# An attention, mixture and gated-unit kernel on one core: the first gated unit's product scheme is changed

## The chip, the core and the metric

The kernel runs on one core of a Trainium2 chip. The metric is the device time of one execution in microseconds (us), median of several. The core has five engines that each take their own row of instructions in order and wait for each other through semaphores: TensorE (PE, matmuls into PSUM banks), VectorE (DVE), ScalarE (ACT), GpSimd (POOL) and SyncE (SP, which issues the DMAs).

## What is computed

```python
attn_out = _attn_ref(q, k, v)         # (2, 8, 576, 64), local band plus a pooled path
x = attn_out.transpose(0, 2, 1, 3).reshape(1152, 512)
x = _moe_ref(x, w_gate, w1, w2)       # 8 experts, 512 -> 1024 -> 512, relu
a = x @ w_a                           # 512 -> 1536
b = x @ w_b
return a * b @ w_out                  # 1536 -> 512
```

All of it is float32. The change touches the last three lines, the gated layer.

## The kernel before

A float32 product is made of three reduced-precision ones: each operand is split into a high part and the rest (`xh`, `xl` for tokens, `hi`, `lo` of a weight block), and hi·hi, hi·lo and lo·hi are added up in PSUM.

The 1152 tokens are handled in two chunks of 512 and 640 columns (`CN` is half of each: 256 and 320). The experts' 16 half units and the gated layer's 6 units follow one another; each unit makes its hidden values with 256 + 256 weight columns and then adds its share of the output, one output tile for each 128 tokens (`o_tile`, `o_mm`).

A unit's first product is a 2x2 block product, with the weights in blocks of depth and columns and the tokens in blocks B11, B12, B21, B22. `g_chunk` does it with seven products in the Strassen-Winograd manner (`PRODUCTS`): combinations of the weight blocks (A11, S1 to S4, A12, A22, made by `queue_combined` on POOL) times blocks or combinations of the tokens (T1 to T4, made by `combine_x`). T2, T3 and T4 lie in `Th`, `Tl`; T1 overwrites the place of B12 in `xh`, `xl`. The results are put together by DVE from PSUM banks and buffers `G`; for a gated unit `a` and `b` are multiplied, and the product is split into `gh` (ACT) and `gl` (POOL).

Between the experts and the gated layer the accumulators are transposed by PE (`t_step`), split into `xh` and `xl`, and kept unsplit as well (tiles `xh_`, `xl_`, `xt_` in the instruction lists), from which `transposed` queues the sums T1 to T4 of each chunk. Before, the second chunk's sums are queued in two parts, one ahead of the last tile's transposes and one after them.

The order of the work is set while the program is written out. PE's products are written in order; between them `pump` takes tasks from queues (`tq` the sums, `wq` the weight pieces, `dq` an earlier decoding), as a small model of the engines' times allows, and each engine executes its row in the order that results. Weight blocks lie in a ring of 13 slots; a slot is used again when its block's uses are done. Raw weights pass through two staging buffers (`raw`), and the next load is issued when a buffer's last use is written out. An eviction of a result frees its PSUM bank; the products of a unit go round six banks, the output tiles round two.

Of the kernel before, what the change touches and what calls it, by code (L numbers as in the profile page):

```python
# [8 lines left out]
F32 = mybir.dt.float32  # L9
# [4 lines left out]
ALU = mybir.AluOpType  # L14
# [5 lines left out]
def attn_moe_glu_kernel(  # L20
# [134 lines left out]
    def run(q):  # L155
        t = q.pop(0)
        t.fn()
        return t
# [75 lines left out]

    def queue_plain(u):

        u.w = {}
        rs = halves(u.load1, (2, 2))
        for i in range(2):
            for j in range(2):  # L240
                def piece(i=i, j=j):
                    b = u.w[i, j] = new_block(NB * 2)
                    split(b, rs[j].tile[:, :, 256 * i:256 * i + 256], 2)
                    rs[j].used()
                wq.append(Task(piece, 0.68, ready=rs[j].ready, slot=True))
# [370 lines left out]
    def g_chunk(u, c, glu=False):  # L616
# [44 lines left out]
        for a, b, bk in PRODUCTS:  # L661
# [47 lines left out]
            yield  # L709


    PLACES = {5: (1, 2, 3, 4, 5), 4: (1, 3, 4, 5), 3: (1, 4, 5)}
# [7 lines left out]
    def phase(u, c, tiles, glu=False, places=None):  # L720

        places = places or PLACES[len(tiles)]
        for i, _ in enumerate(g_chunk(u, c, glu)):
            gate_step()
            for t, at in zip(tiles, places):
                if at == i:
                    t()
                    gate_step()
# [382 lines left out]
    with tc.manual_schedule():  # L1111
# [59 lines left out]
        def close_attention():  # L1171
# [20 lines left out]
            for u in glu_g:  # L1192
                queue_combined(u)
                queue_out(u, 2)
# [135 lines left out]

        def transposed(c, part=None):
            x0, x1 = keep[c]
            where = {"t1": x0[:, 0:2], "b12": x1[:, 0:2], "b22": x1[:, 2:4], "b21": x0[:, 2:4]}
            tq.extend(combine_x(c, lambda name: where[name], (v, g, g, v), None, part))

        for t, tt in enumerate(TILES[1]):
            o_tile(units[last], 1, t)
# [6 lines left out]
            else:  # L1344
                for _ in t_step(TILES[1][t - 1], keep):
                    pass
                if t == 4:
                    transposed(1, slice(0, 192))
        while tq:
            run(tq)  # L1350

        def last_step():
            for _ in t_step(TILES[1][-1], keep, "o"):
                pass
            transposed(1, slice(192, 320))

        phase(glu_g[0], 0, [last_step], True, (0,))
        while tq:
            run(tq)
        phase(glu_g[0], 1, o_tiles(glu_g[0], 0), True)  # L1360
        for g_ in range(1, GU):
# [34 lines left out]
```

## Time and profile before

| what | value |
|---|---|
| median of 3 runs | 1136.14 us |
| the runs | 1133.69 to 1141.28 us |
| the profiled execution | 1141.77 us |
| its span | 1140.0 us |
| PE busy | 1097.3 us, 96% of the span |
| DVE, POOL, ACT busy | 804.1, 541.6, 459.0 us |
| granted clock of PE, mean over the run | 0.974 |

The profile is of one execution. A line of a timeline is one instruction or a few merged; matmuls overlap, so the distance between two starts is the time that one needs, and its own duration is longer. The idle time in brackets is the engine's, and behind it stands what ended it. The granted clock is a share of 2.4 GHz.

### The profile page before, as it was taken

How to read it: one execution, taken by the hardware profiler on the slowest of the kernel's cores; microseconds unless marked ns; L12 is line 12 of the kernel's file. 1: busy time of each engine (PE TensorE's matmuls, PEld its weight loads, DVE VectorE, ACT ScalarE, POOL GpSimd, SP SyncE). 2: the span in 40 equal slices, each digit the busy share in tenths (PEclk: the TensorE clock that was granted, in tenths of full speed). 3: DMA queues.
4: the chain of work that ended last, by engine and by line, in shares of the span. 5: the costliest groups of instructions: out<-in, count | busy, mean ns of one | idle time of the engine just before them, and what ended most of it. 6: DMA issues, size and time to landing. Idle time of an engine off the chain costs nothing.

```text
span 1140.0 us, 18222 instructions
## 1 busy us (share of the span) xinstructions
PE 1097.3 (96%) x6545; PEld 994.1 (87%) x6545; DVE 804.1 (71%) x1593; ACT 459.0 (40%) x1203; POOL 541.6 (48%) x540
## 2 busy tenths in 40 slices
PE   8998999979999999999999999999999979999998
PEld 6897898768889999899998999989899778999997
DVE  6566453777878878778787788877754665666764
ACT  5555442344344443444434444344443532323321
POOL 3312312475355464554645646456453334546431
PEclk9599999989999999999999999999999989999999
DMA  6243200112322323323233132331310101011102
GB/s 168 52 130 101 65 16 1 38 66 65 100 97 75 118 71 120 99 66 118 85 114 97 62 118 84 114 97 61 109 54 22 38 19 37 20 56 56 56 20 83
DMA packets 80841, 84.51 MB, mean 74 GB/s; under 512 B 35952, under 2 KB 54384, under 8 KB 80752
## 3 DMA queue, kind: packets, MB, share of 16 engines
q1 hardware_dynamic: 80752, 83.36, 23.9%
q8 instruction: 51, 0.84, 0.3%
q14 instruction: 38, 0.31, 0.1%
HBM read 71.54 MB, written 11.80 MB: 73 GB/s over the span
## 4 chain that ended last, share of the span: by engine, by line
PE 88%; DVE 6%; ACT 2%; POOL 2%; issue 1%; DMA 0%; DVEq 0%; SPq 0%; POOLq 0%; ACTq 0%
PE g L60 82%; PE at L60 4%; DVE w L135 1%; DVE G L647 1%; ACT p L905 1%; PE at L936 1%; ACT Th L587 0%; DVE xt L581 0%; DVE tgh L581 0%; POOL vd L821 0%; POOL tgh L573 0%; DVE G L657 0%; PE g L734 0%; POOL p L920 0%; PE at L833 0%
## 5 line engine op out<-in xcount | busy, mean ns | idle before, releaser
L60 PE MATMUL g<-w,gh 128*128 128x512 f32 x1314 | 412.6, 395 | 3.9 <-DVE acc L508 1.8
L60 PE MATMUL g<-xh,w 128*128 128x256 f32 (+2 forms) x1472 | 329.9, 305 | 4.5 <-ACT G L683 3.3
L643 POOL TENSOR_TENSOR gl<-G,gh 128x256 fp32r<-128x256 f32 (+1 forms) x216 | 182.5, 853 | 276.6 <-ACT gh L641 265.4
L60 PEld LDWEIGHTS g<-w,gh 128*128 128x128 f32 x1314 | 237.8, 190 | 44.3 <-DVE acc L508 2.0
L60 PE MATMUL g<-w,gl 128*128 128x512 f32 x657 | 258.9, 394 | 0.0
L60 PEld LDWEIGHTS g<-xh,w 128*128 128x128 f32 x1472 | 249.5, 191 | 9.9 <-ACT G L683 3.5
L60 PE MATMUL g<-Th,w 128*128 128x256 f32 (+1 forms) x960 | 214.5, 300 | 14.3 <-DVE G L647 7.0
L60 PE MATMUL g<-xl,w 128*128 128x256 f32 (+2 forms) x736 | 223.3, 303 | 0.5 <-POOL xl L978 0.5
L135 DVE TENSOR_TENSOR w<-raw,w 128x512 fp32r<-128x512 f32 x138 | 134.8, 984 | 106.4 <-ACT w L134 106.4
L647 DVE TENSOR_TENSOR G<-g,G 128x256 f32<-128x256 f32 (+1 forms) x400 | 164.6, 449 | 34.7 <-PE g L60 23.0
L60 PEld LDWEIGHTS g<-Th,w 128*128 128x128 f32 x960 | 164.3, 193 | 19.8 <-DVE G L647 8.3
L639 ACT ACTIVATE G<-G 128x256 f32<-128x256 f32 (+1 forms) x168 | 74.4, 443 | 215.9 <-DVE G L647 215.2
L60 PEld LDWEIGHTS g<-w,gl 128*128 128x128 f32 x657 | 124.4, 189 | 27.1
L60 PEld LDWEIGHTS g<-xl,w 128*128 128x128 f32 x736 | 140.5, 191 | 5.1 <-POOL xl L978 1.0
L60 PE MATMUL g<-Tl,w 128*128 128x256 f32 (+1 forms) x480 | 143.6, 299 | 0.3 <-DVE Tl L594 0.3
L641 ACT CAST gh<-G 128x256 fp32r<-128x256 f32 (+1 forms) x216 | 93.6, 433 | 108.5 <-DVE G L657 91.6
L134 ACT CAST w<-raw 128x512 fp32r<-128x512 f32 x181 | 108.2, 619 | 40.1 <-POOL raw L259 36.5
L508 DVE SCALAR_TENSOR_TENSOR acc<-g,P,acc 128x512 f32<-128x512 f32 x126 | 93.7, 744 | 30.0 <-PE g L60 28.7
L60 PEld LDWEIGHTS g<-Tl,w 128*128 128x128 f32 x480 | 92.3, 192 | 3.8 <-DVE Tl L594 0.7
L389 POOL TENSOR_TENSOR dec<-dec 128x384 f32<-128x384 f32 x48 | 49.8, 1037 | 76.1 <-DVE dec L386 65.7
L259 POOL TENSOR_TENSOR raw<-raw 128x512 f32<-128x512 f32 x40 | 54.5, 1363 | 42.0 <-DVE w L135 25.5
L259 POOL TENSOR_TENSOR s<-raw 128x512 f32<-128x512 f32 x40 | 65.6, 1640 | 1.0 <-DMA raw<-w 0.7
(171 smaller groups left out, 1209.6 us busy)
## 6 DMA issues: line engine op xcount, KB each, us to landing
raw<-in_moe_w_dram SPq DMA_DIRECT2D x128, 256.0 KB
w<-dec SPq DMA_DIRECT2D x48, 192.0 KB
dec<-in_moe_w_a_dram SPq DMA_DIRECT2D x16, 384.0 KB
dec<-in_moe_w_b_dram SPq DMA_DIRECT2D x16, 384.0 KB
dec<-in_moe_w_out_dram SPq DMA_DIRECT2D x16, 384.0 KB
raw<-w SPq DMA_DIRECT2D x48, 128.0 KB
raw<-w SPq DMA_DIRECT2D x12, 256.0 KB
vw<-in_v_dram SPq DMA_DIRECT2D x72, 35.0 KB
```

Source lines behind the costliest of these rows:

```text
L60: nc.tensor.matmul(out=o, lhsT=l, rhs=r, start=start, stop=stop, skip_group_check=not check)
L134: nc.scalar.copy(out=hi, in_=raw)
L135: (low or nc.vector).tensor_tensor(out=lo, in0=raw, in1=hi.bitcast(F32), op=ALU.subtract)
L259: nc.gpsimd.tensor_tensor(out=o(), in0=A(*a), in1=A(*b), op=op)
L389: nc.gpsimd.tensor_tensor(out=tf, in0=tf, in1=mf, op=ALU.add)
L508: nc.vector.scalar_tensor_tensor(out=a, in0=ps, scalar=P[:, tt, u.e:u.e + 1], in1=a, op0=ALU.mult, op1=ALU.add)
L639: nc.scalar.activation(out=src, in_=src, func=AF.Relu)
L641: nc.scalar.copy(out=h, in_=src)
L643: nc.gpsimd.tensor_tensor(out=l, in0=src, in1=h.bitcast(F32), op=ALU.subtract)
L647: nc.vector.tensor_tensor(out=o, in0=bank_, in1=b, op=ALU.add)
L905: nc.scalar.activation(out=p[:, c], in_=sl[:, c * W:(c + 1) * W], func=AF.Exp, bias=nm[:, c:c + 1], scale=1.0, accum_out=rs[:, c:c + 1],)
L936: nc.tensor.transpose(pt[0:W, c * 128:(c + 1) * 128], p[:, c], ident)
```

## The change

The first gated unit (`glu_g[0]`) is done by a new function, `g_whole`, with eight plain block products: for each half of the weight columns and each half of the tokens, `a` and `b` are accumulated over the whole depth in 12 matmuls each. It uses `xh` and `xl` directly and no T. Its weights are queued by `queue_plain` in four plain blocks with eight uses each, not in seven combinations. The sums T1 to T4 of both chunks are queued whole and taken by `pump` while this unit is under way; the two tasks that write T1 (over B12) are held back in `late` until the unit has read that chunk. The other gated units stay as they were. `phase` chooses the function by the unit's blocks, with other places for the output tiles.

```diff
--- before.py
+++ after.py
@@ -232,14 +232,14 @@
         lq.extend(rs)
         return rs
 
-    def queue_plain(u):
+    def queue_plain(u, uses=6):
 
         u.w = {}
         rs = halves(u.load1, (2, 2))
         for i in range(2):
             for j in range(2):
                 def piece(i=i, j=j):
-                    b = u.w[i, j] = new_block(NB * 2)
+                    b = u.w[i, j] = new_block(uses)
                     split(b, rs[j].tile[:, :, 256 * i:256 * i + 256], 2)
                     rs[j].used()
                 wq.append(Task(piece, 0.68, ready=rs[j].ready, slot=True))
@@ -708,6 +708,53 @@
                 finish(0, 0, 0, G4[:, :n], True)
             yield
 
+    def g_whole(u, c, glu=False):
+
+        n = CN[c]
+        us = n / 960 + 0.165
+        aus = n / 1200 + 0.17
+        pus = n / 460 + 0.23
+        for i in range(2):
+            force(lambda: (i, 1) in u.w)
+            for j in range(2):
+                cols = HALF[c][j]
+                for fi in range(2):
+                    p = bank("g")[:, :n]
+                    k = 0
+                    for kt in range(KT):
+                        w = u.w[i, kt // 2]
+                        o = (kt % 2) * 256 + fi * 128
+                        a_h, a_l = w.hi[:, o:o + 128], w.lo[:, o:o + 128]
+                        for lt, rt in ((a_h, xh), (a_h, xl), (a_l, xh)):
+                            mm(p, lt, rt[:, kt, cols], k == 0, k == 3 * KT - 1)
+                            k += 1
+                    M.pe += 12 * (n / 2400 + 0.0135)
+                    for x in range(2):
+                        u.w[i, x].use()
+                    pump()
+                    f = i if glu else i * 2 + fi
+                    sl = slice(j * n, (j + 1) * n)
+                    h, l = GH[c][f][:, sl], GL[c][f][:, sl]
+                    t = G3[i][j][:, :n]
+                    if not glu:
+                        nc.scalar.activation(out=h, in_=p, func=AF.Relu)
+                        act(aus)
+                        nc.vector.scalar_tensor_tensor(
+                            out=l, in0=p, scalar=0.0, in1=h.bitcast(F32), op0=ALU.max, op1=ALU.subtract
+                        )
+                        dve(us)
+                    elif fi == 0:
+                        nc.scalar.copy(out=t, in_=p)
+                        act(aus)
+                    else:
+                        nc.vector.tensor_tensor(out=t, in0=p, in1=t, op=ALU.mult)
+                        dve(us)
+                        nc.scalar.copy(out=h, in_=t)
+                        act(aus)
+                        nc.gpsimd.tensor_tensor(out=l, in0=t, in1=h.bitcast(F32), op=ALU.subtract)
+                        pool(pus)
+                yield
+
 
     PLACES = {5: (1, 2, 3, 4, 5), 4: (1, 3, 4, 5), 3: (1, 4, 5)}
 
@@ -719,8 +766,9 @@
 
     def phase(u, c, tiles, glu=False, places=None):
 
-        places = places or PLACES[len(tiles)]
-        for i, _ in enumerate(g_chunk(u, c, glu)):
+        whole = hasattr(u, "w")
+        places = places or ((0, 1, 2, 2, 3)[5 - len(tiles):] if whole else PLACES[len(tiles)])
+        for i, _ in enumerate((g_whole if whole else g_chunk)(u, c, glu)):
             gate_step()
             for t, at in zip(tiles, places):
                 if at == i:
@@ -1190,7 +1238,10 @@
                 queue_combined(u)
                 queue_out(u)
             for u in glu_g:
-                queue_combined(u)
+                if u is glu_g[0]:
+                    queue_plain(u, 8)
+                else:
+                    queue_combined(u)
                 queue_out(u, 2)
             hold[0] = False
             for r in coming:
@@ -1328,11 +1379,15 @@
             [spare_tile(i, F32, f"xt{i}")[:, 0:KT * 320].rearrange("p (k n) -> p k n", k=KT) for i in range(2)],
         ]
 
-        def transposed(c, part=None):
+        def transposed(c):
             x0, x1 = keep[c]
             where = {"t1": x0[:, 0:2], "b12": x1[:, 0:2], "b22": x1[:, 2:4], "b21": x0[:, 2:4]}
-            tq.extend(combine_x(c, lambda name: where[name], (v, g, g, v), None, part))
-
+            tasks = combine_x(c, lambda name: where[name], (v, g, g, v), None)
+            tasks[0].ready = lambda t=M.pe: M.pe >= t + 3.0
+            tq.extend(tasks[:-2])
+            late.extend(tasks[-2:])
+
+        late.clear()
         for t, tt in enumerate(TILES[1]):
             o_tile(units[last], 1, t)
             if t == 0:
@@ -1344,20 +1399,18 @@
             else:
                 for _ in t_step(TILES[1][t - 1], keep):
                     pass
-                if t == 4:
-                    transposed(1, slice(0, 192))
-        while tq:
-            run(tq)
 
         def last_step():
             for _ in t_step(TILES[1][-1], keep, "o"):
                 pass
-            transposed(1, slice(192, 320))
+            transposed(1)
 
         phase(glu_g[0], 0, [last_step], True, (0,))
+        tq[:0] = late[:2]
+        phase(glu_g[0], 1, o_tiles(glu_g[0], 0), True)
+        tq.extend(late[2:])
         while tq:
             run(tq)
-        phase(glu_g[0], 1, o_tiles(glu_g[0], 0), True)
         for g_ in range(1, GU):
             phase(glu_g[g_], 0, o_tiles(glu_g[g_ - 1], 1), True)
             phase(glu_g[g_], 1, o_tiles(glu_g[g_], 0), True)
```

PE's row at the start of the first gated unit, before (`g_` and a number is a PSUM bank's content, `w_` a weight block, `acc_87` the last token tile):

```order
L60 MATMUL g_9466<-xl,w_9152 128x256
L60 MATMUL g_9466<-xh,w_9152 128x256
L734 MATMUL g_9475<-ident,acc_87 128x128 x4
L60 MATMUL g_9483<-Th,w_9186 128x256
L60 MATMUL g_9483<-Tl,w_9186 128x256
L60 MATMUL g_9483<-Th,w_9186 128x256 x2
L60 MATMUL g_9483<-Tl,w_9186 128x256
L60 MATMUL g_9483<-Th,w_9186 128x256
L60 MATMUL g_9490<-Th,w_9186 128x256
```

and now:

```order
L60 MATMUL g_9449<-xl,w_9152 128x256
L60 MATMUL g_9449<-xh,w_9152 128x256
L782 MATMUL g_9468<-ident,acc_87 128x128 x4
L60 MATMUL g_9476<-xh,w_9107 128x256
L60 MATMUL g_9476<-xl,w_9107 128x256
L60 MATMUL g_9476<-xh,w_9107 128x256 x2
L60 MATMUL g_9476<-xl,w_9107 128x256
L60 MATMUL g_9476<-xh,w_9107 128x256
```

The last tile's transposes now stand after 24 products, and behind them products with `xh` where products with `Th` stood.

POOL's row in the second chunk of the first gated unit, before (`s_` is a combination buffer):

```order
L594 TENSOR_TENSOR Tl<-xt_9296,Th 128x2x128
L594 TENSOR_TENSOR Tl<-xt_9295,Th 128x2x128
L259 TENSOR_TENSOR s_9644<-raw 128x512
L643 TENSOR_TENSOR gl_2968<-G_9292,gh_2966 128x320
L259 TENSOR_TENSOR raw<-raw 128x2x256
L643 TENSOR_TENSOR gl_2968<-G_2449,gh_2966 128x320
L643 TENSOR_TENSOR gl_2968<-G_2445,gh_2966 128x320
L259 TENSOR_TENSOR raw<-raw 128x2x256
L643 TENSOR_TENSOR gl_2968<-G_2447,gh_2966 128x320
L135 TENSOR_TENSOR w_9775<-raw,w_9775 128x512
L135 TENSOR_TENSOR w_9792<-raw,w_9792 128x512
L135 TENSOR_TENSOR w_9807<-s_9644,w_9807 128x512
```

and now:

```order
L594 TENSOR_TENSOR Tl<-xt_9296,Th 128x2x320
L135 TENSOR_TENSOR w_9615<-raw,w_9615 128x512
L754 TENSOR_TENSOR gl_2968<-G_2444,gh_2966 128x320
L135 TENSOR_TENSOR w_9648<-raw,w_9648 128x512
L754 TENSOR_TENSOR gl_2968<-G_2445,gh_2966 128x320
L135 TENSOR_TENSOR w_9664<-s_9246,w_9664 128x512
L259 TENSOR_TENSOR s_9681<-raw 128x512
L754 TENSOR_TENSOR gl_2968<-G_2446,gh_2966 128x320
L135 TENSOR_TENSOR w_9718<-s_9681,w_9718 128x512
L259 TENSOR_TENSOR s_9768<-raw 128x512
L754 TENSOR_TENSOR gl_2968<-G_2447,gh_2966 128x320
```

Pieces of the second unit (`w_9615` to `w_9718`), its combination S4 (`s_9681`) and the third unit's first combination (`s_9768`) now stand between the first unit's `gl`.

DVE's row at the end of the first gated unit, before:

```order
L1294 COPY acc_88<-g_9705 128x512
L647 TENSOR_TENSOR G_2444<-g_9610,G_2444 128x320
L647 TENSOR_TENSOR G_2445<-g_9617,G_2445 128x320
L657 TENSOR_TENSOR G_2445<-G_2444,G_2445 128x320
L1294 COPY acc_89<-g_9730 128x512
L135 TENSOR_TENSOR w_9750<-raw,w_9750 128x512
L647 TENSOR_TENSOR G_2446<-g_9647,G_2446 128x320
L647 TENSOR_TENSOR G_2447<-g_9654,G_2447 128x320
L657 TENSOR_TENSOR G_2447<-G_2446,G_2447 128x320
L135 TENSOR_TENSOR w_9795<-raw,w_9795 128x512
L647 TENSOR_TENSOR G_2446<-g_9778,G_2444 128x256
```

and now:

```order
L135 TENSOR_TENSOR w_9686<-raw,w_9686 128x512
L750 TENSOR_TENSOR G_2446<-g_9695,G_2446 128x320
L1345 COPY acc_82<-g_9711 128x512
L1345 COPY acc_88<-g_9722 128x512
L135 TENSOR_TENSOR w_9757<-raw,w_9757 128x512
L135 TENSOR_TENSOR w_9760<-raw,w_9760 128x512
L750 TENSOR_TENSOR G_2447<-g_9744,G_2447 128x320
L1345 COPY acc_89<-g_9773 128x512
L594 TENSOR_TENSOR xl<-xt_9296,xh 128x2x320
L647 TENSOR_TENSOR G_2446<-g_9799,G_2444 128x256
L647 TENSOR_TENSOR G_2447<-g_9806,G_2445 128x256
```

The two pieces `w_9757` and `w_9760` are the second unit's output weights; the product `G_2447` that frees the bank `g_9744` stands behind them, and T1 of the second chunk (`xl<-xt_9296`) behind that.

## Rows read from the trace of the kernel before

**Rows 1.** PE's waits from 905 to 960 us: in total, times, longest.

```profile
PE g L60 <- ACT Th L587: 4.5, 2, 2.3
```

**Rows 2.** PE's timeline, first gated unit: start, duration, operation, [idle before <-releaser].

```profile
907.46 0.36 PE L60 MATMUL g<-xh,w 128*128 128x256 f32 x1
...
911.87 0.38 PE L60 MATMUL g<-Th,w 128*128 128x256 f32 x1 [2.30 <-ACT Th L587]
...
919.15 0.58 PE L60 MATMUL g<-xh,w 128*128 128x256 f32 x1 [3.28 <-ACT G L683]
...
931.51 0.63 PE L60 MATMUL g<-Th,w 128*128 128x320 f32 x1 [2.19 <-ACT Th L587]
...
936.38 0.50 PE L60 MATMUL g<-w,gh 128*128 128x512 f32 x1 [1.05 <-DVE w L135]
```

**Rows 3.** PE's timeline, entry to the second gated unit.

```profile
950.44 0.43 PE L60 MATMUL g<-xh,w 128*128 128x320 f32 x2
...
954.06 0.39 PE L60 MATMUL g<-Th,w 128*128 128x256 f32 x1 [1.88 <-ACT w L134]
...
955.42 0.80 PE L60 MATMUL g<-Th,w 128*128 128x256 f32 x2 [0.85 <-POOL w L135]
...
959.54 0.28 PE L60 MATMUL g<-xh,w 128*128 128x256 f32 x1
...
960.97 0.63 PE L60 MATMUL g<-w,gh 128*128 128x512 f32 x2
```

**Rows 4.** Stretches: busy us and instructions per engine, PE's clock, DMA share, GB/s.

```profile
872.00:874.00 2.00, 2.00 (x12) 1.78 (x11) 0.64 (x1) 0.00 (x0) 0.00 (x0) 1.00 0.75 214
920.00:925.00 5.00, 5.00 (x27) 5.00 (x27) 2.42 (x6) 1.26 (x3) 1.09 (x2) 0.55 0.01 3
959.50:1000.00 40.50, 40.50 (x259) 37.56 (x258) 26.54 (x46) 11.75 (x27) 19.89 (x19) 1.00 0.18 56
```

**Rows 5.** PE's timeline, two groups of 320-column products and an output tile, full clock.

```profile
937.64 0.30 PE L60 MATMUL g<-xh,w 128*128 128x320 f32 x1
...
941.15 0.63 PE L60 MATMUL g<-w,gh 128*128 128x512 f32 x2
...
942.54 0.31 PE L60 MATMUL g<-Th,w 128*128 128x320 f32 x1
```

**Rows 6.** DVE's timeline, the sums of the transposed tokens.

```profile
894.23 2.48 DVE L739 TENSOR_TENSOR xl<-g,xh 128x512 fp32r<-128x512 f32 x4 [0.30 <-ACT xh L738]
...
911.14 0.69 DVE L581 TENSOR_TENSOR xh<-xh,xl 128x512 f32<-128x512 f32 x1
...
914.17 1.63 DVE L581 TENSOR_TENSOR xt<-xt,xt 128x384 f32<-128x384 f32 x1
915.84 0.56 DVE L581 TENSOR_TENSOR xt<-xt 128x384 f32<-128x384 f32 x1
```

**Rows 7.** POOL's timeline at the same place.

```profile
913.66 1.73 POOL L594 TENSOR_TENSOR Tl<-xh,Th 128x512 fp32r<-128x512 f32 x1
```

**Rows 8.** ACT's timeline, the copy of A11's result in the first gated unit.

```profile
918.74 0.64 ACT L683 COPY G<-g 128x256 f32<-128x256 f32 x2
```

**Rows 9.** POOL's groups by shape, 959.5 to 1120 us: count, busy us, mean ns.

```profile
L643 POOL TENSOR_TENSOR gl<-G,gh 128x256 fp32r<-128x256 f32 x20 | 14.8, 738 | 44.4 <-ACT gh L641 43.6 <-PE g L60 0.8
L643 POOL TENSOR_TENSOR gl<-G,gh 128x320 fp32r<-128x320 f32 x16 | 14.5, 909 | 27.8 <-ACT gh L641 27.7
L259 POOL TENSOR_TENSOR s<-raw 128x512 f32<-128x512 f32 x9 | 13.3, 1480 | 0.9 <-DMA raw<-w 0.7
L135 POOL TENSOR_TENSOR w<-s,w 128x512 fp32r<-128x512 f32 x9 | 12.6, 1401 | 3.4 <-ACT w L134 3.4
```

**Rows 10.** POOL's groups by shape, 185 to 260 us.

```profile
L594 POOL TENSOR_TENSOR Tl<-tgl,Th 128x640 fp32r<-128x640 f32 x1 | 2.2, 2166 | 0.0
```

**Rows 11.** SyncE's queue: two issues of raw gated weights.

```profile
870.43 1.90 SPq L431 DMA_DIRECT2D raw<-w  x4
...
936.95 1.90 SPq L431 DMA_DIRECT2D raw<-w  x4
```

## The prediction

> **What bounds the kernel now.** TensorE (PE) is busy 96% of the span (the table ahead), so two things can move the end much: PE's idle time and the number of its products. I read PE's waits next, stretch by stretch: from 300 to 905 us and from 960 us on the view lists none. Between 905 and 960 us it lists six, and the longest sum is for ScalarE (ACT) casts of Th, the transposed tokens' sums [rows 1]. That is the first gated unit and the entry to the second, where the diff works. Then PE's own timeline there. The first unit starts at 907.46 us; PE stands still before the products with Th (2.30), before xh (3.28), before Th of the second chunk (2.19) and before a weight block (1.05) [rows 2]. The second unit, from 950.59 us (its predecessor's last 320-column product starts at 950.44 and takes 0.15), stands still before S2·T2, 1.88 and 0.85 [rows 3]. The price is more than idle time: from 920 to 925 us the granted clock averages 0.55, mostly the lower of the two levels (1.2 GHz), and PE does 27 products in 5 us, where at 0.119 each it needs 3.2; from 959.5 to 1000 us the clock is 1.00 and PE busy throughout [rows 4].
>
> Why PE waits: VectorE (DVE), ACT and GpSimd (POOL) take their rows in order, and the second factors of the seven products, T1 to T4, are sums that can only be made once the tokens are transposed. ACT's copy of A11's result, which frees PSUM banks, started at 918.74 us, behind the casts of those sums [rows 8]: that is the 3.28.
>
> **Added: 24 products.** Seven products of half the depth are 84 matmuls a chunk; the eight block products are 2x2x2 groups of 12, which is 96. At full clock 12 products of 256 columns take 1.43 us (959.54 to 960.97) [rows 3], 12 of 320 take 1.755 (24 from 937.64 to 941.15), an output tile of six 512-column products 1.39 [rows 5]. So the addition is 1.43 + 1.76 = 3.2 us, all on PE; nothing hides it.
>
> **Removed: the unit's dependence on T1 to T4.** The new first unit reads xh and xl alone, and the four subtractions that finish them for its first chunk end at 896.7 us [rows 6], eleven us before it begins. With no wait its length is 8 x 1.43 (first chunk) + 0.5 (the last tile's transposes) + 8 x 1.76 (second chunk) + 4 x 1.39 (output tiles) = 31.6 us; now it is 43.1 (907.46 to 950.59). That gives 11.5 us, the 3.2 already paid.
>
> **Moved: the weight blocks.** Plain blocks need no combinations on POOL, four slots of the ring instead of seven, and both halves of the staging area come free after four casts with a DVE subtraction each. So the second half of the second unit's raw weights, now loaded at 936.95 us [rows 11], can load before the first unit begins, and its blocks can be cut while the first unit multiplies: the two waits before S2·T2 lose their cause. From 950.59 to the end of the first output tile at 959.54 PE takes 8.95 us, where 2 x 1.43 + 1.39 = 4.25 would do: 4.7 us. That POOL and DVE do fewer operations for these blocks lies beside PE's work and counts nothing. **Sum without any new wait: 11.5 + 4.7 = 16.2 us.**
>
> **What the sums cost in their new place.** All T's are now made while PE does the 31.6 us, between the unit's own results. In that time POOL's row holds 19 instructions: four gl of 256 and four of 320 columns, four weight pieces, two s and one raw combination, and four Tl. By the means of the later units, which already contain what DVE does to POOL, the first five kinds take 4 x 0.74 + 4 x 0.91 + 4 x 1.40 + 3 x 1.48 = 16.6 us [rows 9]; with 2 x 1.73 for the smaller Tl [rows 7] and 2 x 2.17 for the larger [rows 10] it is 24.4 us, so POOL is three quarters full, in order. DVE has 13 operations with two SBUF inputs there. One of 512 elements takes 0.69 alone and one of 384 takes 0.56, but 1.63 where it started beside POOL's Tl, which itself took 1.73 [rows 6, 7]. So I take it that the two engines exclude each other in such operations. Thirteen of them by 0.68 to 0.82 (640 elements, continued from the two rows) are 9.6 us; with POOL's 24.4, which holds part of the mutual waiting already, the 31.6 us are about full.
>
> The Trainium skill says it more sharply (SBUF — State Buffer, section "SBUF: two separate sides"): a GpSimd instruction and a VectorE instruction with two SBUF inputs share a pair of ports, and whoever starts first holds it for the whole instruction. This speaks against putting the sums here; rows 6 and 7 agree with it. By it the wait worked out below stands; were it otherwise, that wait would be nothing.
>
> I followed the rows of the new order with these durations from 907.46 us on. Of the first chunk, each result leaves its bank four us or more before the sixth bank after it needs the place, and gl of the chunk's first columns is ready at about 925 us, where the first output tile wants it at 926.6. The first place that fails is the end of the second chunk. POOL makes the combination S4 (s_9681) only at about 939 us. The load of the second unit's output weights waits for that staging half. As many bytes issued at 870.43 [rows 11] were through by about 874.2, with the DMA engines 75% busy from 872 to 874 us [rows 4]; so this load lands at about 942.9. Two casts and two DVE subtractions follow, to 944.8, and behind them in DVE's row stands the product that frees the bank of g_9744: 945.3 us. PE wants that bank for the second half of S1·T1 at 939.0 + 1.43 + 1.43 + 1.39 + 0.72 = 944.0. A wait of 1.3, with 0.15 to fill the pipeline 1.5 us. From below it is 0: if POOL and DVE overlap, S4 is made at 933 and nothing is late. From above: POOL another 4 us late makes 5.3 us of waiting and a stretch at the low clock like that from 920 us, 1.8 more [rows 4], so 7.1. I take 1.5, the end nearer to the later units, where the same engines do the same work and PE waits for nothing.
>
> **Forecast: 16.2 - 1.5 = 14.7 us.** The profiled execution took 1141.77 us and would take 1127.1. It stands 5.6 us above the median of the runs; nothing says that this difference lies in the stretch, so I take the gain off the median: 1136.14 - 14.7 = **1121.4 us**.
>
> **Rivals.**
> (a) The backlog is larger. For it: three quarters of POOL's time, with s_9768 of the third unit, which needs a load of its own, ahead of a gl, and DVE and ACT in order behind the output weights' load. Against it: seven blocks of the first unit with their combinations are no longer made. Gain 16.2 - 7.1 = 9.1, time 1127.
> (b) The unit does not end the waiting, it passes it on. T1 overwrites tokens and may be written only after the unit has read them; if T1, T3 or T4 came after the second unit wants them, the waits for sums (2.30 + 3.28 + 2.19) and a stretch at the low clock (1.8) would reappear there: gain 16.2 - 9.6 = 6.6, time 1129.5. Against it: the second unit wants T2 at 940.5 us, 29 us after the last of its sums began in the trace of before (911.14) [rows 6].
> (c) Slower: the prefetch never recovers. A load that SyncE may issue only once POOL has made S4 stands ahead of casts, and these ahead of results; if each unit hands its delay to the next, every chunk from the second unit on has an entry like the present one, 4.7 us. Ten chunks follow, so 47 - 11.5 = 35.5 us slower, about 1172; it decides from the third such chunk on (2.4 x 4.7 = 11.5). Against it: from 959.5 to 1000 us POOL is busy 19.9 of 40.5 us [rows 4], so a delay can be worked off within a unit.
>
> **How the numbers follow.** Forecast, gains from 11.5 to 17: 0.68. (a), gains of 7 to 11.5: 0.20. (b): 0.07. (c): 0.05. The range takes in the forecast and (a), from 1136.14 - 16.2 = 1119.9 to 1127, widened by some 3 us on both sides for the scatter of the three runs (1133.69 to 1141.28): 1117 to 1130. A change of 1% is 11.4 us, about what this measurement can tell from none. Faster by more: the forecast and a little that scatter lends (a), 0.70. Within 1%: most of (a), and (b), 0.25. Slower: (c), 0.05.
>
> **What would show it.** In the changed profile PE's timeline should run from 907 to about 939 us without a wait at clock 1.00, also from 920 to 925 us. The second unit should begin 11.5 us sooner than now. A short wait for a DVE product should stand in its S1·T1, and none for a weight block before S2·T2. Wrong would be: a wait for gl in the first output tiles, POOL waiting at s_9768 for a DMA ahead of a gl, or waits that come back in later units.

## The result and the profile after

The changed kernel took 1124.06 us (median of 4 runs, 1115.49 to 1127.49), the kernel before 1135.76 us beside it (4 runs, 1133.69 to 1141.28): 11.7 us less. The ratio on record is 0.9876, 95% interval 0.983 to 0.9923; it and the ratios below are given as the record has them, and are not the quotients of the medians (here 0.9897). The time lies in the forecast's range, 2.7 us above its 1121.4. The profiled execution took 1115.49 us with a span of 1113.7, so it is the fastest of the four, as that of before (1141.77) was one of the slowest of its kernel. The two profiles differ by 26.3 us, which is far more than the change did, and the text below has to take them apart.

First the change's own place. PE's timeline after, at the first gated unit and the entry to the second, to be read against [rows 2, 3]:

```profile
897.78 0.37 PE L60 MATMUL g<-xh,w 128*128 128x256 f32 x1
...
900.73 0.60 PE L782 MATMUL g<-ident,acc 128*128 128x128 f32 x4
...
916.85 0.63 PE L60 MATMUL g<-w,gh 128*128 128x512 f32 x2
...
929.42 0.28 PE L60 MATMUL g<-xh,w 128*128 128x256 f32 x1
...
930.83 0.29 PE L60 MATMUL g<-Th,w 128*128 128x256 f32 x1
...
933.59 0.28 PE L60 MATMUL g<-xh,w 128*128 128x256 f32 x1
```

No line carries an idle time in brackets any more. The first unit lasts from 897.78 to 929.42, 31.64 us (43.13 before); from the second unit's first product to the end of its first output tile, 929.42 to 933.59, it is 4.17 us (8.95 before). The view of waits confirms it: from 250 us to the end it lists these two lines only, and PE's timeline has their last wait at 279.45 us.

```profile
PE g L60 <- DVE acc L508: 1.8, 1, 1.8
PE g L60 <- DVE G L647: 0.9, 2, 0.6
```

Stretches of the same execution, busy time of PE, its weight loads, DVE, ACT and POOL, then PE's granted clock, against [rows 4]:

```profile
897.00:910.00 13.00, 13.00 (x109) 12.87 (x108) 9.45 (x14) 5.96 (x13) 4.36 (x4) 1.00 0.00 1
910.00:915.00 5.00, 5.00 (x36) 5.00 (x36) 4.47 (x5) 3.16 (x7) 4.95 (x4) 1.00 0.00 0
915.00:929.00 14.00, 14.00 (x85) 13.05 (x84) 6.84 (x9) 6.61 (x15) 13.02 (x11) 1.00 0.13 41
929.00:940.00 11.00, 11.00 (x76) 10.16 (x75) 7.78 (x12) 4.41 (x10) 6.25 (x6) 1.00 0.32 92
```

PE is busy throughout at clock 1.00, the 2.4 GHz level, where before there was 0.55. POOL's 22.3 us of the 32 from 897 to 929 (4.36 + 4.95 + 13.02) are near the forecast's 24.4 of 31.6, and yet nothing waits for it.

A measure that leaves out what happens earlier in the kernel is the time from the first gated unit's first product to the end of the span. It is 1140.0 - 907.46 = **232.54 us** before and 1113.7 - 897.78 = **215.92 us** after. I call it the tail below. The change's own gain is so 16.6 us; the remaining 9.7 us between the two profiles had arisen before 897.78 us, where PE does the same products in both kernels.

### The profile page after: what moved, and what is told of

It reads as the page before. It is cut to its first block, busy times and chain, and to the rows that moved or that the text cites. A ratio compares the mean times of both kernels' runs of the same rounds, so it can differ in the third digit from the quotient of the medians.

```text
span 1113.7 us, 18218 instructions
## 1 busy us (share of the span) xinstructions
PE 1081.4 (97%) x6569; PEld 980.8 (88%) x6569; DVE 800.4 (72%) x1568; ACT 457.1 (41%) x1198; POOL 530.1 (48%) x530
## 4 chain that ended last, share of the span: by engine, by line
PE 88%; DVE 4%; POOL 3%; ACT 2%; issue 1%; DMA 1%; SPq 0%; DVEq 0%; POOLq 0%; ACTq 0%
PE g L60 83%; PE at L60 4%; ACT p L953 1%; POOL p L968 1%; DVE w L135 1%; PE at L984 0%; POOL vd L869 0%; DMA dec<-in_moe_w_a_dram 0%; POOL rawv L866 0%; DVE tgh L581 0%; POOL tgh L573 0%; PE g L782 0%; ACT w L134 0%; ACT pd L957 0%; POOL Tl L594 0%
## 5 line engine op out<-in xcount | busy, mean ns | idle before, releaser
L60 PE MATMUL g<-xh,w 128*128 128x256 f32 (+2 forms) x1536 | 340.1, 303 | 1.3 <-DVE G L647 0.6
L643 POOL TENSOR_TENSOR gl<-G,gh 128x256 fp32r<-128x256 f32 (+1 forms) x208 | 175.6, 853 | 272.4 <-ACT gh L641 260.4
L60 PEld LDWEIGHTS g<-xh,w 128*128 128x128 f32 x1536 | 258.0, 190 | 6.5 <-ACT xh L1025 1.0
L60 PE MATMUL g<-xl,w 128*128 128x320 f32 (+2 forms) x768 | 231.7, 302 | 0.5 <-POOL xl L1026 0.5
L135 DVE TENSOR_TENSOR w<-raw,w 128x512 fp32r<-128x512 f32 x139 | 141.0, 1024 | 108.2 <-ACT w L134 108.1
L60 PE MATMUL g<-Th,w 128*128 128x320 f32 (+1 forms) x912 | 200.4, 296 | 6.9 <-DVE G L647 6.9
L647 DVE TENSOR_TENSOR G<-g,G 128x256 f32<-128x256 f32 (+1 forms) x380 | 156.7, 450 | 28.2 <-PE g L60 13.3
L60 PEld LDWEIGHTS g<-Th,w 128*128 128x128 f32 x912 | 153.4, 190 | 11.5 <-DVE G L647 8.7
L60 PE MATMUL g<-Tl,w 128*128 128x256 f32 (+1 forms) x456 | 134.8, 296 | 0.0
L60 PEld LDWEIGHTS g<-Tl,w 128*128 128x128 f32 x456 | 86.3, 189 | 2.9
```

The costliest lines, as they stand in the source:

```text
L60: nc.tensor.matmul(out=o, lhsT=l, rhs=r, start=start, stop=stop, skip_group_check=not check)
L135: (low or nc.vector).tensor_tensor(out=lo, in0=raw, in1=hi.bitcast(F32), op=ALU.subtract)
L643: nc.gpsimd.tensor_tensor(out=l, in0=src, in1=h.bitcast(F32), op=ALU.subtract)
L647: nc.vector.tensor_tensor(out=o, in0=bank_, in1=b, op=ALU.add)
```

## Experiments

The questions were four: why the medians moved by 11.7 us and the tail by 16.6; whether the gain is the missing wait for sums, the earlier weight blocks, or both; whether the chain over S4 that the forecast charged 1.5 us for is real; and whether DVE and POOL excluding each other costs anything here. The tails, of one profiled execution each (the kernels from `sums_first` on were run once):

| kernel | first product | span | tail | time, us |
|---|---|---|---|---|
| before | 907.46 | 1140.0 | 232.54 | 1141.77 |
| after | 897.78 | 1113.7 | 215.92 | 1115.49 |
| `again` | 907.58 | 1123.6 | 216.02 | 1125.35 |
| `after_warm` | 898.72 | 1114.7 | 215.98 | 1116.46 |
| `before_warm` | 899.67 | 1132.2 | 232.53 | 1133.93 |
| `after_warm5` | 899.78 | 1115.7 | 215.92 | 1117.50 |
| `sums_first` | 898.03 | 1115.5 | 217.47 | 1117.65 |
| `two_plain` | 898.26 | 1117.4 | 219.14 | 1119.23 |
| `s4_plus2` | 900.93 | 1117.7 | 216.77 | 1119.75 |
| `s4_plus5` | 899.04 | 1120.2 | 221.16 | 1122.34 |
| `tl_on_dve` | 905.58 | 1121.5 | 215.92 | 1123.30 |
| `late_blocks` | 898.13 | 1115.7 | 217.57 | 1117.94 |
| `late_blocks_end` | 898.35 | 1124.0 | 225.65 | 1126.10 |

(The last column is that of the profiled execution.) Where nothing behind the opening is edited, the tail repeats within 0.1 us, in the four such executions of the changed kernel and the two of before, so a difference of 0.5 us in it means something, while the whole time scatters by 10.

### Where the medians' scatter comes from

`again` is the changed kernel without an edit.

> The changed kernel once more, five rounds. Theory A: the change is worth 16 to 17 us in one place, from the first product of the first gated unit to the end (232.5 us before, 215.9 us in the profile after), and all that differs from that between medians is the opening of the program, where the granted clock from 25 to 50 us was 0.60 in the profile before and 1.00 in the profile after by chance. So the place takes 215.9 us within 0.5 in this profile too, the runs scatter by 10 us or so with their clock, and the median gain is between 11 and 20 us. Rival B: the gain is smaller than 16, because the profile after was a lucky one in its last part: then the place takes 219 to 222 us here.

1120.38 us (6 runs, 1115.74 to 1125.35) beside 1135.25 of before (17 runs, 1131.92 to 1144.31); ratio 0.9845, 0.9806 to 0.9884. Its profiled execution was one of the long ones, and its windows of the opening (the attention part) against those of the first profile after show why. `again`:

```profile
0.00:25.00 25.00, 20.39 (x149) 17.76 (x150) 14.98 (x57) 13.23 (x54) 8.52 (x23) 0.93 0.73 181
25.00:50.00 25.00, 23.11 (x127) 21.30 (x125) 13.77 (x49) 13.33 (x57) 10.61 (x18) 0.60 0.19 40
```

and after:

```profile
0.00:25.00 25.00, 20.53 (x148) 17.85 (x149) 14.97 (x57) 13.44 (x55) 8.53 (x23) 0.93 0.69 179
25.00:50.00 25.00, 21.40 (x188) 19.23 (x186) 18.81 (x66) 16.91 (x72) 13.51 (x21) 1.00 0.30 72
```

Until 25 us the two executions of the same program agree. From 25 to 50 us the granted clock is 0.60 in one and 1.00 in the other, and PE does 127 products instead of 188. The first gated unit then begins 9.8 us later. The profile of before also has 0.60 there, and its first product stands at 907.46, where `again` has 907.58. Not all of it stems from these 25 us: PE's same product stands about 8.2 us later in the profile of before at 104 us, and 9.7 us later from 194 us on. The rest arises near 190 us, where both long executions have a granted clock of 0.84 (185 to 196 us) and the first profile after has 1.00. Since `again` is the changed kernel and shows the same, the 9.7 us between the two profiles are the clock of an execution, and not the change.

If so, holding the opening's clock up in both kernels must leave the tail's difference alone. The opening has products of constants whose results nobody reads, 3 in each early step; these two kernels have 8. `after_warm` and `before_warm` have the same edit, of the changed kernel and of the kernel before:

```diff
-    WARM = (16, 3)
+    WARM = (16, 8)
```

> The changed kernel with eight dummy matmuls in place of three at each step of the opening. Theory A: if the low clock of the opening is what scatters the runs, the mean clock from 25 to 100 us rises to 0.97 or more in this profile and the runs lie within 4 us of each other; the place from the first gated product to the end stays at 215.9 us. The time is then either about 1116 us, or higher by what the dummy matmuls themselves cost PE (some 40 steps by 5 products of 0.11 us, at most 22 us, if none of it is hidden). Rival B: the scatter stays as it is, and has another cause than the opening's clock.

> The kernel before with the same eight dummy matmuls. Theory A: with the opening alike in both, the difference between this and the changed kernel with eight is 16 to 17 us, the place's own gain, with little scatter. Rival B: the difference stays at 11 to 13 us, the gain of the medians, and the change loses some 4 us elsewhere.

The opening's granted clock was 1.00 in all four windows from 0 to 100 us in both. `after_warm`: 1116.71 us (6 runs, 1116.27 to 1118.82), ratio 0.9818 (0.9787 to 0.9849). `before_warm`: 1134.03 us (12 runs, 1131.68 to 1135.08), ratio 0.9975 (0.9952 to 0.9998). The scatter of the changed kernel fell from 9.6 to 2.6 us. The tails still differ by 16.6 us (232.53 and 215.98), and the two medians by 17.3. In the profiles the first gated unit begins 0.95 us later in `before_warm`: both wait 1.8 us for the same DVE copy near 280 us, and behind it the granted clock is 0.84 over 10 us in `before_warm` and 1.00 in `after_warm`.

`after_warm5` takes 5:

```diff
-    WARM = (16, 3)
+    WARM = (16, 5)
```

> The changed kernel with five dummy matmuls at each step of the opening, between the three of the change and the eight of the earlier run. If the opening's clock is what scatters the runs, five lie between the two: median 1114.5 to 1118 us if five are enough to hold the clock (they cost PE less than eight), 1117 to 1121 with a scatter of some 8 us if not.

1114.13 us (4 runs, 1113.73 to 1117.50) beside 1135.14 of before (7 runs); ratio 0.9802, 0.9771 to 0.9833. This is the lowest median of all runs, a little under the 1114.5 to 1118 that was expected. The kernel before was run beside it; the changed kernel without the edit was run on other chips, and so was that with 8, so neither what 5 gain over 3 nor whether 5 or 8 is better can be told from these runs. In its profile the granted clock was 0.93 from 25 to 50 us, and not 1.00 as with 8.

### What the moved sums and the plain unit are worth

`sums_first` keeps the plain unit, but makes all sums of a chunk except T1 ahead of the next product, as a unit would need that wants them at once.

```diff
             transposed(1)
+            while tq:
+                run(tq)
 
+        while tq:
+            run(tq)
         phase(glu_g[0], 0, [last_step], True, (0,))
```

> The place of the sums undone: all sums of a chunk are written out ahead of the next product of the first gated unit, which still reads no T. Theory A (what counts is that PE does not read the sums): the engines that free the banks stand behind the sums, at most some 6 us, while six banks cover 8 us of products, so PE waits for 0 to 2 us in the first chunk and the place from the first gated product to the end takes 216 to 218.5 us. Rival C (what counts is where the sums stand in the rows of DVE and ACT): PE waits as before, 3 us and more at the first chunk's later products with low clock behind them, and the place takes 220 us or more.

PE waits once, for an ACT copy that frees a bank and stands behind the sums' casts, the kind of wait that [rows 2, 8] show:

```profile
911.40 0.41 PE L60 MATMUL g<-xh,w 128*128 128x320 f32 x1 [1.18 <-ACT G L747]
```

The tail is 1.55 us longer. So most of the first unit's gain does not need the sums to be spread: it is there because the unit no longer reads them.

`two_plain` makes the second gated unit plain too; T1 of each chunk is written behind its products there.

```diff
-                if u is glu_g[0]:
+                if u in glu_g[:2]:
                     queue_plain(u, 8)
...
         phase(glu_g[0], 0, [last_step], True, (0,))
-        tq[:0] = late[:2]
         phase(glu_g[0], 1, o_tiles(glu_g[0], 0), True)
-        tq.extend(late[2:])
...
             phase(glu_g[g_], 0, o_tiles(glu_g[g_ - 1], 1), True)
+            if g_ == 1:
+                tq[:0] = late[:2]
             phase(glu_g[g_], 1, o_tiles(glu_g[g_], 0), True)
+            if g_ == 1:
+                tq.extend(late[2:])
...
```

> The second gated unit is done with eight products too, so the price of the 24 added products is paid once more, and there is no wait left that it could remove. Theory: the place from the first gated product to the end grows by 3.2 us, from 215.9 to 219.1, and PE still waits for nothing. Rival: the products cost nothing in the end, since PE's idle time elsewhere takes them up: 216 us. Or the fewer weight pieces on POOL and DVE give something back: below 218.

No wait, and the tail is 3.22 us longer. That is the price of 24 more products by itself (the forecast's sum for it was 1.43 + 1.76 = 3.2), and it shows that nothing was left to be gained at the second unit's entry: its sums are in time.

### What the earlier weight blocks are worth

`late_blocks` holds the second unit's first weight piece back until the second output tile of the first unit's second chunk is written, `late_blocks_end` until the fourth, behind the unit's last product. Both by one gate (shown for `late_blocks`; `late_blocks_end` calls `held[3]` in place of `held[1]`):

```diff
+        gate = [False]
...
+                    first_ = len(wq)
                     queue_combined(u)
+                    if u is glu_g[1]:
+                        wq[first_].ready = lambda r=wq[first_].ready: gate[0] and r()
...
+        held = o_tiles(glu_g[0], 0)
+
+        def open_gate():
+            held[1]()
+            gate[0] = True
...
-        phase(glu_g[0], 1, o_tiles(glu_g[0], 0), True)
+        phase(glu_g[0], 1, [held[0], open_gate] + held[2:], True)
```

> The weight blocks of the second gated unit may be begun only after the second output tile of the first unit's second chunk, about 25 us after the unit's first product, while in the changed kernel the first is begun before that unit. The sums and the first unit stay as changed. Theory I (the early blocks are a part of the gain of their own, 4.7 us by the prediction): PE waits again for blocks at the second unit's first products, 4 to 9 us with low clock after it, and the place takes 219 to 226 us; the first unit itself shows no wait. Rival J: the waits before S2·T2 came from the sums on POOL, not from late blocks: no wait, 216 us.

The tail is 1.65 us longer, less than the 3 to 10 that I had thought: one wait, before S2·T2,

```profile
932.57 0.50 PE L60 MATMUL g<-Th,w 128*128 128x256 f32 x2 [0.98 <-POOL w L135]
```

and the clock stayed at 1.00. By the end of the first output tile that has cost 1.3 us; the other 0.4 were not traced. What this kernel leaves as it is are the raw weights, which still load early, and the pieces start 1.1 us after the second unit (POOL at 930.85, the unit at 929.76).

> The second gated unit's first weight pieces are held back until the last product of the first unit is written, two products later than in the run that held them until the second output tile (1.65 us). That the place of the weights is worth some 4.7 us: the combinations and pieces now stand on GpSimd behind the last result's rest, which ends about 33 us after the first product; with one combination (1.3), two more (2.6) and the piece (1.3) the second block is cut some 5 us after TensorE wants it, and the next ones follow every 1.3 to 1.7 us; waits of 4 to 7 us before the second unit's first products, a granted clock well under 1.00 behind them, and the stretch from the first product of the first unit to the end at 220 to 226 us (215.92 in the changed kernel). That the weights' place is worth little, and the gain came from the missing sums alone: the stretch at 216 to 218 us, as with the smaller delay.

PE's waits at the second unit's entry, all of which name a weight block:

```profile
931.04 0.39 PE L60 MATMUL g<-xh,w 128*128 128x256 f32 x1 [0.90 <-ACT w L134]
...
934.41 0.80 PE L60 MATMUL g<-xh,w 128*128 128x256 f32 x2 [2.87 <-DVE w L135]
...
937.95 0.58 PE L60 MATMUL g<-Th,w 128*128 128x256 f32 x1 [1.03 <-ACT w L134]
...
939.30 0.80 PE L60 MATMUL g<-Th,w 128*128 128x256 f32 x2 [0.56 <-POOL w L135]
```

and the stretches there:

```profile
931.00:935.00 4.00, 1.09 (x4) 0.89 (x5) 3.35 (x2) 0.00 (x0) 3.23 (x3) 0.68 0.01 2
935.00:940.00 5.00, 3.40 (x14) 2.82 (x14) 0.00 (x0) 3.34 (x7) 2.80 (x3) 0.50 0.00 0
940.00:945.00 5.00, 5.00 (x28) 4.64 (x28) 2.14 (x4) 0.00 (x0) 3.00 (x3) 0.74 0.11 39
```

The tail is 9.73 us longer: 5.36 us of waits, and most of the other 4.4 from products at a granted clock of 0.50 to 0.74. The 2.87 has a part that I had not seen: DVE makes T1 of the second chunk first (`xl<-xt`, 1.90 us beside POOL's combinations) and the first weight piece behind it (1.75). With the pieces early, somewhat late and last, the entry costs nothing, 1.65 and 9.73; before the change it cost 8.95 - 4.17 = 4.8, between these.

### The chain over S4

The forecast charged 1.5 us for the chain from POOL's combination S4 over a load to the DVE product that frees a bank for S1·T1. To see whether the chain exists and how much it has to spare, S4 of the second unit is computed three times (`s4_plus2`) and six times (`s4_plus5`, with `range(5)`), into the same buffer:

```diff
-        comb("S4", (0, 1), (0, 0), ALU.subtract, s3, (0, 1), None)
+        def s3_slow():
+            o = s3()
+            if u is glu_g[1]:
+                for _ in range(2):
+                    nc.gpsimd.tensor_tensor(out=o, in0=A(0, 1), in1=A(0, 0), op=ALU.subtract)
+            return o
+
+        comb("S4", (0, 1), (0, 0), ALU.subtract, s3_slow, (0, 1), None)
```

In the changed kernel itself the chain reads so: POOL's S4, SyncE's issue, ACT's two casts, DVE's subtractions and the product behind them.

```profile
924.71 1.30 POOL L259 TENSOR_TENSOR s<-raw 128x512 f32<-128x512 f32 x1
926.03 0.81 SPq L409 DMA_DIRECT2D raw<-w  x2
928.72 1.34 ACT L134 CAST w<-raw 128x512 fp32r<-128x512 f32 x2 [1.74 <-DMA raw<-w]
929.37 1.41 DVE L135 TENSOR_TENSOR w<-raw,w 128x512 fp32r<-128x512 f32 x2 [3.96 <-ACT w L134]
930.70 0.48 DVE L750 TENSOR_TENSOR G<-g,G 128x320 f32<-128x320 f32 x1
```

The order is the one that the forecast described, but the product ends at 931.18, and PE wants its bank at 933.59 + 0.72 = 934.3: 3.1 us to spare.

> The combination S4 of the second unit is made three times in place of once on POOL, with the same result, so that everything behind it on POOL is 2.6 to 3.5 us later. Theory D, from the trace after: the product that frees PE's bank ended at 931.2 us and PE wanted the bank at 934.3, so there is 3.1 us to spare. PE then waits for 0 to 0.5 us, the place takes 215.9 to 216.5 us. Rival E: the chain from S4 by the load of the output weights to that product does not reach PE at all, because DVE makes up for it: no wait in this run nor in the next.

The tail is 0.85 us longer, a little over the 0.6 at most that was expected. The product ended 36.2 us after the unit's first, 2.8 later than without the edit and just in time; the wait that appears, 0.55 us at 941.69, names a copy that stands behind it and frees an output tile's bank:

```profile
941.69 0.74 PE L60 MATMUL g<-w,gh 128*128 128x512 f32 x2 [0.55 <-DVE acc L1352]
```

> S4 is made six times, so what stands behind it is 6.5 to 8.7 us later. Theory D: 3.1 us of that is covered, and PE waits for 3.4 to 5.6 us in the second unit's S1 product for the DVE product behind the output weights, with some low clock after it: the place takes 219.5 to 224 us. Rival E: no wait, 216 us. Rival F: POOL's own later row (gl of the first unit's second half) is what PE waits for, in an output tile of the second unit, not in S1.

Here the wait stands where the forecast put it, in the second half of S1·T1:

```profile
939.31 0.38 PE L60 MATMUL g<-xh,w 128*128 128x256 f32 x1 [3.08 <-DVE G L757]
```

```profile
939.00:943.00 4.00, 3.69 (x13) 3.12 (x14) 3.01 (x6) 2.15 (x5) 2.96 (x3) 0.60 0.48 137
```

The tail is 5.24 us longer: 3.08 and 0.23 of waits (the shorter for a `gl` of POOL, in an output tile), and 1.9 at a granted clock of 0.60 behind them, in which an output tile took 2.56 us instead of 1.39. The chain is real; the change has 3.1 us to spare at this bank, and the copy behind it begins to cost when the chain is 2.8 us later (`s4_plus2`).

### DVE beside POOL

DVE's sums of the second chunk in the changed kernel, each of 640 elements, and what POOL did there:

```profile
907.08 0.81 DVE L581 TENSOR_TENSOR xt<-xt,xt 128x640 f32<-128x640 f32 x1
907.93 1.25 DVE L581 TENSOR_TENSOR xt<-xt 128x640 f32<-128x640 f32 x1
909.21 1.80 DVE L581 TENSOR_TENSOR xt<-xt,xt 128x640 f32<-128x640 f32 x1
...
908.46 1.87 POOL L594 TENSOR_TENSOR Tl<-xh,Th 128x512 fp32r<-128x512 f32 x1
910.29 1.87 POOL L259 TENSOR_TENSOR raw<-raw 128x512 f32<-128x512 f32 x1
```

The same operation took 0.81 us where it started with POOL idle and 1.80 where it started beside POOL's Tl. That Tl ended at 910.33, and the sum 0.68 us later, at 911.01; POOL's combination, begun at 910.29, ended 1.15 us after that, where such a one takes 1.30 alone. So the two did this work one after the other. The rule of the Trainium skill (SBUF — State Buffer, section "SBUF: two separate sides"), that the engine that starts first holds a shared pair of ports for its whole instruction, agrees with these durations. What it costs was tried by giving POOL's four Tl to DVE:

```diff
-    def combine_x(c, tmp, low, tot, part=None):
+    def combine_x(c, tmp, low, tot, part=None, low_on=None):
...
-                e.tensor_tensor(out=l, in0=get(key), in1=h.bitcast(F32), op=ALU.subtract)
+                (low_on or e).tensor_tensor(out=l, in0=get(key), in1=h.bitcast(F32), op=ALU.subtract)
...
-            tasks = combine_x(c, lambda name: where[name], (v, g, g, v), None)
+            tasks = combine_x(c, lambda name: where[name], (v, g, g, v), None, None, v)
```

> The four Tl of the first gated unit's stretch, made by POOL, are made by DVE at the same place of the program; all other rows stay as they were. Theory G (the two engines exclude each other in operations with two SBUF inputs): in the trace after, DVE's four 640-element sums took 0.81, 1.25, 1.80 and 1.58 us where 0.82 is the time alone, and POOL's Tl 1.30 to 2.16. With Tl gone from POOL (6.9 us there) and 3.0 us more on DVE, the sums' excess over 0.82 shrinks from 2.2 us to under 1.2, S4 is made 2 to 4 us sooner than 926.0 - 897.8 = 28.2 us after the first product, and the place still takes 215.9 us, since PE waited for nothing. Rival H (each engine slows the other by sharing, or the long times are waits for POOL's Th casts): the sums keep their lengths. Rival: DVE is late now and PE waits.

The tail is 215.92 us, as without the edit, though four of POOL's operations (1.30, 1.87, 2.16 and 1.57 us) were gone. I had expected S4 two to four us sooner; it ended 28.4 us after the first product, where the changed kernel has 28.2. POOL's row has waits now:

```profile
920.62 1.20 POOL L754 TENSOR_TENSOR gl<-G,gh 128x256 fp32r<-128x256 f32 x1 [1.89 <-ACT gh L752]
923.35 0.74 POOL L754 TENSOR_TENSOR gl<-G,gh 128x256 fp32r<-128x256 f32 x1 [1.54 <-ACT gh L752]
...
930.15 0.89 POOL L754 TENSOR_TENSOR gl<-G,gh 128x320 fp32r<-128x320 f32 x1 [1.52 <-ACT gh L752]
```

It waits for ACT's casts of the unit's results, and the last of these waits stands two operations ahead of S4. These results came later by way of DVE, which multiplies `a` and `b` and now makes the Tl as well. For the second result of 320 columns, in the changed kernel and in this run:

```profile
916.70 0.31 PE L60 MATMUL g<-xh,w 128*128 128x320 f32 x1
920.01 0.48 DVE L750 TENSOR_TENSOR G<-g,G 128x320 f32<-128x320 f32 x1
...
924.50 0.31 PE L60 MATMUL g<-xh,w 128*128 128x320 f32 x1
929.10 0.48 DVE L750 TENSOR_TENSOR G<-g,G 128x320 f32<-128x320 f32 x1
```

DVE's product begins 3.0 us after PE's last one ends in the changed kernel, and 4.3 us after it in this run. In the changed kernel itself POOL stood still for nothing from 907.7 to 928.1 us, so there S4 came when the work ahead of it in POOL's row was done. `tl_on_dve` moved work from one to the other of two engines that take turns in it, and S4 came no sooner; what the exclusion costs is not shown by it. The sums' time beyond 0.81 us each fell from 2.2 to 1.4 us in all (0.81, 1.25, 1.81 and 0.81; under 1.2 was expected), the 1.81 now beside POOL's combination of 1.88.

## Why the prediction came out as it did

**What bounds the kernel: right.** PE bound it, and both of the things named, idle time and products, moved the end as priced. Of the 16.6 us in the tail, 43.13 - 31.64 = 11.5 are the first unit (forecast 11.5), 8.95 - 4.17 = 4.8 the second unit's entry (forecast 4.7); together 16.3, where the sum without a new wait said 16.2. The last 0.35 us lie behind the first output tile and were not traced. The forecast took off 1.5 of its 16.2 for a new wait, so its 14.7 is 1.9 under the tail's gain.

**Added products: right.** `two_plain` pays 3.22 us for another 24 (forecast 3.2), with no wait that could hide in it.

**Why PE waited: right.** A wait for an ACT copy behind the sums' casts comes back as soon as these stand ahead of the next product (`sums_first`, 1.18 us).

**Weight blocks: right in the mechanism and the size** (4.8 against 4.7), the mechanism shown by the two doses of lateness. That the second half's raw weights load before the first unit begins is in SyncE's queue after, against the issue at 936.95 in [rows 11]:

```profile
867.23 12.38 SPq L431 DMA_DIRECT2D raw<-w  x8
```

Its last four issues start at 877.72 us, 20 us ahead of the unit.

**The sums in their new place: the chain right, its size wrong.** The wait of 1.5 us was 0, the lower end that the forecast gave it. From the unit's first product the forecast counted 31.5 us to S4, 3.9 for the load, and 37.8 to the product; measured were 28.2 to S4's end, 2.7 from issue to cast, and 33.4. PE wanted the bank at 36.5 in both. The load was costed from one that went in four issues of 128 KB within 1.90 us [rows 11]; this one went in two of 256 KB within 0.81 us. The larger error is the 3.3 us at S4. It doesn't lie in the durations: up to S4's end POOL did 15 operations in 20.6 us, and the forecast's own prices for these 15 add up to 19.7. It lies in the idle time that the forecast let stand between them, some 11.8 us (31.5 - 19.7), where POOL had 7.6, and that all before 907.7 us. The forecast says that its prices hold part of the mutual waiting of POOL and DVE already; where it put the rest of the idle time, its working doesn't show. The forecast named "S4 at 933 and nothing late" as what would follow if POOL and DVE overlapped. They do not overlap in the sums above; S4 came at the equivalent of 935.7, and that left 3.1 us to spare. The upper end, a wait with 1.8 us of low clock behind it, is like what `s4_plus5` made (waits of 3.3 and 1.9 of low clock, for 5.3 and 1.8).

**From the tail to the median: the step that cost more than the wait.** "Nothing says that this difference lies in the stretch, so I take the gain off the median" was the right choice: the tail of before is 232.54 us in that profile and 232.53 in `before_warm`, which was 7.8 us shorter. But the median of few runs inherits that clock. Off the 1135.76 us that before took beside the changed kernel, the tail's 16.6 would give 1119.1; measured were 1124.06 in four runs and 1120.38 in six. The size of this follows from the two profiles, 9.7 us apart ahead of the first gated unit, most of it by an opening at 0.60 in one and 1.00 in the other; that the unprofiled runs differ in the same window is argued from their mean clocks (0.974 to 0.980 in the three long ones, 0.992 in the short one), not shown. So there is luck in the number: the tail gained 1.9 us more than the forecast, and by this account the openings of the four runs took 4.9 of the gain. The measured gain of 11.7 is just within the gains forecast (11.5 to 17), and just over the 11.4 us (1%) that it called about what this measurement can tell from none.

**Rivals.** (a), a larger backlog, would have a tail 7.1 us longer than without a wait: it was not there. (b) would show waits for sums in the second unit: none, and `two_plain` found nothing to gain there. (c) needs an entry cost at each unit: no wait stands between 279 us and the end. Of the signs that would show the forecast right, the clock of 1.00, the second unit 11.5 us sooner and the missing wait before S2·T2 came; the short wait for a DVE product did not.

## What to carry to other kernels

When a stage waits because its operands are sums that several engines must make first, let the first user take the plain operands, if the extra products (here 3.2 us) cost less than the waits and the low clock that follows them (11.5 and 4.8 us back); the sums are then made beside its products. That an engine is three quarters full in a stage is no delay by itself. Follow the one chain that ends at the bounding engine, and find how much later it could end; here it was 3.1 us, and `s4_plus2` and `s4_plus5` showed where that runs out. Where whole times scatter by more than the change, compare a stretch that begins at the change: here it repeated within 0.1 us.

## What was unexpected of the hardware

The same instructions ran the opening with a granted clock of 0.60 or of 1.00 between 25 and 50 us, in different executions of one program; with the shorter stretch near 190 us it decided 9.8 us of 1120. Eight products of constants in each early step instead of three gave 1.00 from 0 to 100 us and runs within 2.6 us of each other, at about 1 us more than the shortest runs without them (median 1116.71 against 1115.49 to 1115.91). In the other direction, 3.1 us in which PE stood still cost 1.9 us more afterwards, and 5.4 us cost some 4 more, since the products behind them ran at 0.50 to 0.74; a single 0.98 us was followed by 1.00. One and the same wait of 1.8 us near 280 us was followed by 1.00 in `after_warm` and by 0.84 over 10 us in `before_warm`.
